# First chunk's last product from split operands, block by block of its weights

## The chip, the cores and the metric

The kernel runs on one core of a Trainium2 chip. The metric is device time in microseconds (us), the median of several executions. A core has five engines that matter here, each with its own queue that it works off in order: TensorE (PE, matmuls; PEld is its weight load), VectorE (DVE), ScalarE (ACT), GpSimd (POOL), and SyncE (SP), which issues the DMAs.

## What is computed

Attention with pooled keys and values, and a gated channel mix behind it, in float32 for 8 batches of 576 positions, 8 heads of 64:

```
k_p = k.reshape(B, H, Sp, pool, D).mean(axis=3)
v_p = v.reshape(B, H, Sp, pool, D).mean(axis=3)
attn = softmax(scale * np.matmul(q, k_p.transpose(0, 1, 3, 2)))
x = np.matmul(attn, v_p)
...
xk = mu_k * x + (1.0 - mu_k) * x_prev
xr = mu_r * x + (1.0 - mu_r) * x_prev
k = np.maximum(xk @ w_k, 0.0)
v = k * k @ w_v
r = 1.0 / (1.0 + np.exp(-(xr @ w_r)))
return (r * v).astype(np.float32)
```

x_prev is x one position earlier. The weights arrive as float64 words; w_k is 512 x 1024, w_v 1024 x 512, w_r 512 x 512.

## The kernel before

The 4608 positions are worked off in 12 chunks of 384, each made of three tiles of 128. A chunk's work: per tile the scores (`softmax`, L620), the normalized probabilities (px for the last 8 keys, L670; pm for the first 64, L676), their transposes on PE (`transposed` L695, `transposed_rest` L740 or L750); per pair of heads the product with the values (`attended`, L794) and the mixing with the position before (`shifted`: ScalarE L807, GpSimd copies L817 to L819, VectorE L826), which gives the operands of the channel mix, two per pair (m = 0 for k, 1 for r); eight blocks of the hidden product with w_k (`hidden`, L870), squared after relu; three gate products with w_r and a sigmoid (`gate`, L919, L926); three last products with w_v (`mixed`, L951), multiplied by the gate (L960) and stored (L964).

Most products are made from split operands: each number is the sum of a high part (rounded to the type float32r by a copy on ScalarE) and a low part (the rest, a subtraction), and three passes (high x high, low x high, high x low) stand for one float32 product. `x_parts` (L842 on ScalarE, L844 on GpSimd) splits the mixed operands, L893 and L895 split the squares (sh and sl), `split` (L491, L494) splits the weights. Chunk 0 alone (WHOLE) is computed from whole float32 operands, since the split weights don't exist yet: one matmul call, which the profile shows as two instructions. Weights are converted from float64 words to float32 by `convert` (L460 on ScalarE; L462, L464, L469 on VectorE), in place of the words, and split into high and low when chunk 0 is through with them: LOW_BY says whether VectorE (v) or GpSimd (g) makes the low part. SUM_BY says who adds up the pooled keys and values (t: PE, by L512; v or g: L501). BY_HEAD lists the tiles whose exponentials ScalarE makes head by head with the sum in the same step (L642); the others take a subtraction (L651), one exponential (L656) and a sum (L658).

`mixed` takes the tiles of a chunk one after the other, each with one PSUM bank ("mm", three of them), over the eight blocks of w_v. In chunk 0 the next tile's product may begin when the first has done its first block, and chunk 1's first hidden product when the third has.

The order in which every engine gets its instructions is set while the program is built, by the class `Order`: each function above is a generator that names the engine it needs next and waits for what it needs; a planner with assumed lengths takes, among those that are ready, the one with the earliest due time. Due times come from formulas at the end of the function (L968 to L998) less or plus an entry of the table EARLIER. What comes out is a fixed queue per engine; nothing is reordered on the chip. LOADS is the order of the first DMAs.

## Time and profile before

| | us |
|---|---|
| median of 3 executions | 631.29 (630.67 to 632.04) |
| the profiled execution | 631.28 |
| its span | 629.5 |
| busy in it: PE, DVE, ACT, POOL | 615.7, 402.1, 354.6, 208.2 |

The span is what the profiler saw from the first to the last instruction; 1.8 us of the execution lie outside it. In the page and the views, a row of a timeline starts with the start and the duration in us, then engine, line, operation, tile written <- tiles read, shape and count; in brackets the idle time of the engine ahead of it and what ended it. Matmuls overlap, so a matmul's own duration is longer than its share of PE: the step from one start to the next tells the share. The same holds for VectorE's rows, whose steps are some 0.08 us shorter than their durations.

### The profile page before, as it was taken

The page shows a single profiled execution, that of the slowest core. Times are in us where ns is not written, and L with a number is a line of the kernel's source. Part 1 is how long each engine was busy: PE and PEld are TensorE (multiplying, and loading weights), DVE is VectorE, ACT ScalarE, POOL GpSimd, SP SyncE. Part 2 cuts the span into 40 slices and gives each one's busy share as a digit, 9 for nine tenths or more (in the row PEclk, how much of TensorE's full clock was granted, in tenths as well). Part 3 has the DMA queues.
Part 4 walks back from the last instruction along what each step waited for, and adds up shares of the span by engine and source line. Part 5 has one row for each costly group of instructions (what it writes and reads, how often), then busy time and mean ns, then how long its engine had stood idle before and what let it go on. Part 6 is the DMA issues. An engine that isn't in the chain of part 4 may idle for free.

```text
span 629.5 us, 8993 instructions
## 1 busy us (share of the span) xinstructions
PE 615.7 (98%) x3210; PEld 533.1 (85%) x3210; DVE 402.1 (64%) x786; ACT 354.6 (56%) x778; POOL 208.2 (33%) x324
## 2 busy tenths in 40 slices
...
GB/s 315 340 403 171 34 35 51 35 76 142 94 51 158 59 51 51 2 143 108 18 18 51 42 187 55 3 18 56 133 98 33 35 18 33 18 2 33 18 2 50
DMA packets 34989, 50.92 MB, mean 81 GB/s; under 512 B 6528, under 2 KB 22912, under 8 KB 34944
## 3 DMA queue, kind: packets, MB, share of 16 engines
...
## 4 chain that ended last, share of the span: by engine, by line
PE 88%; DMA 6%; DVE 5%; SPq 1%; issue 0%; DVEq 0%
PE mm L951 32%; PE mm L870 29%; PE mm L919 14%; PE bank L794 5%; PE sc L620 5%; DMA got_wk<-in_w_k 4%; PE bank L695 2%; DMA got_wv<-in_w_v 1%; DVE tmp L464 1%; DVE got_wr L469 1%; PE bank L750 1%; SPq L421 0%; DVE got_wv L469 0%; DVE tmp L462 0%; DVE ptl L708 0%
## 5 line engine op out<-in xcount | busy, mean ns | idle before, releaser
L870 PE MATMUL mm<-xkh,w_k 128*128 128x384 f32 x704 | 182.3, 339 | 0.0
L951 PE MATMUL mm<-w_v,sh 128*128 128x512 f32 x528 | 171.7, 393 | 0.0
L870 PEld LDWEIGHTS mm<-xkh,w_k 128*128 128x128 f32 x704 | 125.6, 188 | 1.5 <-issue 0.6
L870 PE MATMUL mm<-xkl,w_k 128*128 128x384 f32 x352 | 118.0, 335 | 0.0
L951 PEld LDWEIGHTS mm<-w_v,sh 128*128 128x128 f32 x528 | 99.3, 188 | 19.5
L951 PE MATMUL mm<-w_v,sl 128*128 128x512 f32 x264 | 103.1, 390 | 0.0
L919 PE MATMUL mm<-w_r,xrh 128*128 128x512 f32 x264 | 86.3, 397 | 0.0
L807 ACT ACTIVATE t<-bank,om_sb 128x384 f32<-128x384 f32 x96 | 49.1, 580 | 46.7 <-PE bank L794 46.6
L893 ACT CAST sh<-rk 128x384 fp32r<-128x384 f32 x88 | 45.2, 513 | 51.9 <-DVE rk L887 51.4
L670 POOL TENSOR_TENSOR px<-e,sm 128x64 f32<-128x64 f32 x31 | 9.6, 310 | 189.8 <-DVE sm L664 189.8
L960 DVE TENSOR_TENSOR rs<-mm,rs 128x512 f32<-128x512 f32 x36 | 24.7, 687 | 74.7 <-PE mm L951 74.6
L826 DVE SCALAR_TENSOR_TENSOR xm<-bank,mu_sb,t 128x384 f32<-128x384 f32 x88 | 51.1, 612 | 31.8 <-POOL t L819 15.4
L895 DVE TENSOR_TENSOR sl<-rk,sh 128x384 fp32r<-128x384 f32 x88 | 53.3, 610 | 21.3 <-ACT sh L893 21.2
L870 PEld LDWEIGHTS mm<-xkl,w_k 128*128 128x128 f32 x352 | 66.1, 188 | 0.0
L887 DVE SCALAR_TENSOR_TENSOR rk<-mm,rk 128x384 f32<-128x384 f32 x88 | 48.5, 552 | 22.7 <-ACT rk L880 21.9
L501 POOL TENSOR_TENSOR stage<-stage 128x512 f32<-128x512 f32 (+5 forms) x60 | 52.9, 887 | 25.5 <-DMA stage<-in_vm 14.8
L844 POOL TENSOR_TENSOR xkl<-xm,xkh 128x384 fp32r<-128x384 f32 x44 | 45.5, 1034 | 48.0 <-ACT xkh L842 47.6
L919 PEld LDWEIGHTS mm<-w_r,xrh 128*128 128x128 f32 x264 | 49.7, 188 | 10.1
L951 PEld LDWEIGHTS mm<-w_v,sl 128*128 128x128 f32 x264 | 49.7, 188 | 8.9
L880 ACT ACTIVATE rk<-mm 128x384 f32<-128x384 f32 x88 | 42.9, 487 | 22.1 <-PE mm L870 21.1
L919 PE MATMUL mm<-w_r,xrl 128*128 128x512 f32 x132 | 51.5, 390 | 0.0
L620 PE MATMUL sc<-kbd,qs 128*128 128x144 f32 (+1 forms) x312 | 40.6, 289 | 5.4 <-ACT e L642 3.2
(120 smaller groups left out, 952.8 us busy)
## 6 DMA issues: line engine op xcount, KB each, us to landing
...
```

The lines of the kernel that those rows point to most:

```text
L501: nc_eng.tensor_tensor(out=st[:, :, :w], in0=st[:, :, :w], in1=st[:, :, w:2 * w], op=ALU.add)
L620: nc.tensor.matmul(out=halves[g // 2][o:o + n, 0, k:k + 2 * KEYS], lhsT=qs[:, g, o:o + n], rhs=kbd[b % 2][:, g, :], start=True, stop=True,)
L807: nc.scalar.activation(out=t[:, m, 1:n + 1], in_=xp, func=AF.Copy, scale=om_sb[:, m, g:g + 1])
L826: nc.vector.scalar_tensor_tensor(out=xm[:, :n], in0=xp, scalar=mu_sb[:, m, g:g + 1], in1=t[:, m, :n], op0=ALU.mult, op1=ALU.add,)
L844: nc.gpsimd.tensor_tensor(out=lo, in0=xm[:, :n], in1=hi, op=ALU.subtract)
L870: nc.tensor.matmul(out=hp, lhsT=w[:, o], rhs=x[:, ct, :n], start=(ct == 0 and k == 0), stop=(ct == NCT - 1 and k == len(terms) - 1),)
L880: nc.scalar.activation(out=rk[:, :n], in_=hp, func=AF.Relu)
L887: nc.vector.scalar_tensor_tensor(out=rk[:, :n], in0=hp, scalar=0.0, in1=rk[:, :n], op0=ALU.max, op1=ALU.mult)
L893: nc.scalar.copy(out=sh[:, :n], in_=rk[:, :n])
L895: nc.vector.tensor_tensor(out=operand("sl", c)[:, jt, :n], in0=rk[:, :n], in1=sh[:, :n], op=ALU.subtract)
L919: nc.tensor.matmul(out=bank, lhsT=x[:, ct, o], rhs=w, start=(ct == 0 and k == 0), stop=(ct == NCT - 1 and k == len(terms) - 1),)
L951: nc.tensor.matmul(out=bank, lhsT=s[:, o], rhs=w, start=(jt == 0 and k == 0), stop=(jt == NJT - 1 and k == len(terms) - 1),)
```

## The change

Chunk 0's last product is made from split operands like that of every other chunk: its squares are copied to sh (high) and the rest goes to sl, and the product takes three passes of split w_v. It takes the weights block by block: for each of the eight blocks the three tiles' products are added up, in three PSUM banks at once (`mixed_by_weights`); the output steps of a tile follow its last block (`put_out`). `second` holds the three passes. The hidden and the gate products of chunk 0 stay whole. w_v is split as soon as it is converted, with a tile of its own for each block; the conversion's last step writes to one of two new slots (fv), from which the split reads. Splits of w_k and w_r follow one another by the order of their loads alone, and chunk 1's first hidden product may begin when all of chunk 0's last product is issued. WBUFS falls by eight, for the eight tiles of w_v.

Beside that: tiles 1 and 3 also take their exponentials by head; two of the eight squares of chunk 0 go from ScalarE to VectorE; the low parts of w_r are all GpSimd's, those of w_v VectorE's but one; the sums of k0, v1 and v2 move (k0 to VectorE, v1 to GpSimd, v2 to PE); the order of the first loads and all due times are new.

Where instructions now stand, at three places. In these rows mm, bank and sc are PSUM banks, sh and sl the squares' parts, got_wr and w_r the converted and the split gate weights, w_v the split last weights, pm and px the probabilities, rows of x2 or x4 one row for several.

PE, at the start of chunk 0's last product, before (L740 and L695 transpose tile 5's probabilities, L919 is the gate, L620 the scores of tile 6):

```order
L740 MATMUL bank_113<-ident,pr_95 96x128 x2
L695 MATMUL bank_115<-ident,pm_90 128x128 x4
L919 MATMUL mm_117<-got_wr_249,xrh_363 128x512
L919 MATMUL mm_117<-got_wr_254,xrh_363 128x512
L919 MATMUL mm_117<-got_wr_278,xrh_363 128x512
L919 MATMUL mm_117<-got_wr_289,xrh_363 128x512
L620 MATMUL sc_112<-kbd_70,qs_104 128x144 x4
L951 MATMUL mm_118<-got_wv_293,sh_416 128x512
L951 MATMUL mm_118<-got_wv_306,sh_416 128x512
```

The same place now (L928 is the gate, L631 scores, L706 the transpose of tile 5's pm, L946 the product):

```order
L631 MATMUL sc_114<-kbd_70,qs_106 128x144 x4
L928 MATMUL mm_118<-got_wr_330,xrh_349 128x512
L928 MATMUL mm_118<-got_wr_335,xrh_349 128x512
L706 MATMUL bank_115<-ident,pm_91 128x128 x4
L946 MATMUL mm_120<-w_v_520,sh_426 128x512
L946 MATMUL mm_120<-w_v_520,sl_447 128x512
L946 MATMUL mm_120<-w_v_520,sh_426 128x512
L946 MATMUL mm_119<-w_v_520,sh_426 128x512
```

The transposes of tile 5's pm stood ahead of the last gate product and stand now directly ahead of chunk 0's last product; those of its px (L751) come after the product's seventh block. Further on, the four L805 groups of chunk 1 stand two ahead of the eighth block, one behind it, and one behind the first L881 rows of chunk 1.

VectorE, around tile 5's pm, before (L469 is the last conversion step of a block of w_v):

```order
L464 SCALAR_TENSOR_TENSOR tmp_101<-got_wv_306,tmp_101 128x512
L708 TENSOR_TENSOR ptl_463<-bank_114,pth_462 128x4x128
L670 TENSOR_TENSOR px_93<-e_89,sm_99 128x64
L469 SCALAR_TENSOR_TENSOR got_wv_306<-got_wv_306,tmp_101 128x512
L730 CAST pr_95<-px_93 128x2x32 x2
L676 TENSOR_TENSOR pm_90<-e_89,sm_99 128x512
```

The same place now (L466, L468, L477 are the conversion's steps, L503 the low part of a block of w_v, L512 adds up values, L687 is pm):

```order
L477 SCALAR_TENSOR_TENSOR fv_104<-got_wv_378,tmp_101 128x512
L503 TENSOR_TENSOR w_v_520<-fv_103,w_v_520 128x512
L512 TENSOR_TENSOR stage_108<-stage_108 128x2x256
L477 SCALAR_TENSOR_TENSOR fv_103<-got_wv_374,tmp_102 128x512
L669 TENSOR_REDUCE sm_99<-e_89 128x8
L466 TENSOR_SCALAR tmp_101<-tmp_101 128x512
L672 TENSOR_SCALAR sm_99<-sm_99 128x8
L675 RECIPROCAL sm_99<-sm_99 128x8
L468 SCALAR_TENSOR_TENSOR tmp_101<-got_wv_368,tmp_101 128x512
L681 TENSOR_TENSOR px_93<-e_89,sm_99 128x64
L512 TENSOR_TENSOR stage_108<-stage_108 128x2x128
L687 TENSOR_TENSOR pm_91<-e_89,sm_99 128x512
```

Before tile 5's pm stood behind the second conversion of w_v; now it stands behind the fourth, and behind the low parts of two blocks and all of chunk 0's squares.

GpSimd, at the operands of chunk 1, now (L855 makes low parts, k and r in turn, L681 and L687 are a tile's px and pm):

```order
L855 TENSOR_TENSOR xkl_808<-xm_85,xkh_807 128x384
L855 TENSOR_TENSOR xrl_829<-xm_83,xrh_828 128x384
L826 COPY t_81<-carry 128x2
L828 COPY carry<-t_81 128x2
L830 MEMSET t_81 128x2
L681 TENSOR_TENSOR px_93<-e_89,sm_99 128x64
L687 TENSOR_TENSOR pm_91<-e_89,sm_99 128x512
L826 COPY t_82<-carry 128x2
L828 COPY carry<-t_82 128x2
L830 MEMSET t_82 128x2
L855 TENSOR_TENSOR xkl_808<-xm_84,xkh_807 128x384
L855 TENSOR_TENSOR xkl_808<-xm_83,xkh_807 128x384
```

Two more low parts stand ahead of these rows and two behind, close together; before, the first pair stood alone between splits of w_k, well ahead of the rest.

The diff, with EARLIER cut to a row of each:

```
@@ -27,7 +27,7 @@
-WBUFS = 2 * NJT + NCT + 1
+WBUFS = NJT + NCT + 1
@@ -37,74 +37,74 @@
 REBASE = 2.0 ** -((1023 - 127) // 8)
 
 LOADS = (
-    "k0 k1 q1 q0 q2 wk0 c0 v0 v1 wk1 k3 r0 wk2 q3 wk3 wk4 v3 wk5 r1 q4 v2 wk6 wk7 wr0 wr1 q5 k2 wr2 "
-    "wr3 wv0 wv1 wv2 wv3 wv4 wv5 wv6 wv7 "
+    "k1 k0 q1 q0 wk0 v0 q2 v1 c0 wk1 k3 r0 wk2 q3 wk3 wk4 wk5 r1 v3 wk6 v2 k2 wk7 wr0 q4 wr1 wr2 wr3 "
+    "q5 wv0 wv1 wv2 wv3 wv4 wv5 wv6 wv7 "
 )
 
 SUM_BY = {
-    "k0": "t", "k1": "v", "v0": "t", "v1": "t", "r0": "t", "k2": "v", "k3": "v", "v2": "g", "v3": "v",
+    "k0": "v", "k1": "v", "v0": "t", "v1": "g", "r0": "t", "k2": "v", "k3": "v", "v2": "t", "v3": "v",
     "r1": "g",
 }
 
-NORM_BY = {0: "v", 1: "v", 2: "v", 3: "v", 4: "g", 6: "g", 5: "v"}
+NORM_BY = {0: "v", 1: "v", 2: "v", 3: "v", 4: "g", 6: "v", 5: "v"}
 WARMING = 4
 
-LOW_BY = {"k": "gvgvvvgv", "r": "gvgv", "v": "gvvggvgv"}
-BY_HEAD = (0, 2)
+LOW_BY = {"k": "gvgvvvgv", "r": "gggg", "v": "vvvvgvvv"}
+BY_HEAD = (0, 1, 2, 3)
 
 BESIDE = (1,)
-SQUARED_ON_ACT = 8
+SQUARED_ON_ACT = 6
 COPIES_ON_ACT = 0
 
 EARLIER = {
-    "transposed_rest 6": 4.1, "hidden 2 5": -6.4, "convert r 1": -3.5, "mixed 0 1": -9.9,
...
+    "transposed_rest 6": 28.2, "hidden 2 5": -0.7, "convert r 1": -3.1, "mixed 0 1": 8.4,
...
 }
-SPARE = 2.4
-SECOND = 13.3
+SPARE = 2.6
+SECOND = 15.4
 
@@ -285,7 +285,7 @@
 
     def operand(kind, c):
         if (kind, c) not in operands:
-            dtype = F32 if c in WHOLE and kind != "ptr" else F32R
+            dtype = F32 if c in WHOLE and kind not in ("ptr", "sh", "sl") else F32R
             operands[kind, c] = sb.tile(shapes[kind], dtype, name=f"{kind}_{c}", tag=kind)
         return operands[kind, c]
 
@@ -301,6 +301,7 @@
     slots("vq", 1, [REM, 2, D], F32R)
     slots("tmp", 2, [P, WP])
+    slots("fv", 2, [P, WP])
 
@@ -424,7 +425,10 @@
             return
         if kind[0] == "w":
             yield "sp", 0.6, False
-            got = sb.tile([P, 2 * WP], I32, name=f"got_{kind}{i}", tag="w", bufs=WBUFS)
+            own = kind[1] == "v"
+            got = sb.tile(
+                [P, 2 * WP], I32, name=f"got_{kind}{i}", tag=f"wv{i}" if own else "w", bufs=1 if own else WBUFS
+            )
             held["got", kind[1], i] = got
             nc.sync.dma_start(
                 out=got,
@@ -464,29 +468,34 @@
         nc.vector.scalar_tensor_tensor(
             out=t, in0=top, scalar=-0x80000000, in1=t, op0=ALU.bitwise_and, op1=ALU.bitwise_or
         )
+        to = got[:, :WP]
+        if kind == "v":
+            held["fv", i] = yield take("fv")
+            to = held["fv", i].bitcast(I32)
         yield dve(WP)
-        full[kind, i] = got[:, :WP].bitcast(F32)
+        full[kind, i] = to.bitcast(F32)
         nc.vector.scalar_tensor_tensor(
-            out=got[:, :WP], in0=low_word, scalar=29, in1=t,
+            out=to, in0=low_word, scalar=29, in1=t,
             op0=ALU.logical_shift_right, op1=ALU.bitwise_or,
         )
         order.give("tmp", ff)
         order.make(("full", kind, i))
 
-    order_of = [w[1:] for w in LOADS.split() if w[0] == "w"]
+    order_of = [w[1:] for w in LOADS.split() if w[0] == "w" and w[1] != "v"]
 
     def split(kind, i, *used):
 
         yield need(("full", kind, i), *used)
-        at = order_of.index(kind + str(i))
-        if at > WBUFS - 2 * NJT - NCT - 1:
-            before = order_of[at - (WBUFS - 2 * NJT - NCT)]
-            yield need(("parts", before[0], int(before[1:])))
-        if at:
-            yield need(("splitting", at - 1))
+        own = kind == "v"
+        if not own:
+            at = order_of.index(kind + str(i))
+            if at:
+                before = order_of[at - 1]
+                yield need(("parts", before[0], int(before[1:])))
         yield act(WP)
-        order.make(("splitting", at))
-        both = sb.tile([P, 2, WP], F32R, name=f"w_{kind}{i}", tag="w", bufs=WBUFS)
+        both = sb.tile(
+            [P, 2, WP], F32R, name=f"w_{kind}{i}", tag=f"wv{i}" if own else "w", bufs=1 if own else WBUFS
+        )
         high[kind, i], low[kind, i] = both[:, 0], both[:, 1]
         nc.scalar.copy(out=high[kind, i], in_=full[kind, i])
         v = LOW_BY[kind][i] == "v"
@@ -494,6 +503,8 @@
         (nc.vector if v else nc.gpsimd).tensor_tensor(
             out=low[kind, i], in0=full[kind, i], in1=high[kind, i], op=ALU.subtract
         )
+        if own:
+            order.give("fv", held.pop(("fv", i)))
         order.make(("parts", kind, i))
 
     def halve(nc_eng, st, cols, n):
@@ -872,10 +883,9 @@
                     start=(ct == 0 and k == 0), stop=(ct == NCT - 1 and k == len(terms) - 1),
                 )
         order.make(("hid", c, jt))
-        if c:
-            yield need(("mixed", c - 1), ("early", "sl", 0), ("early", "sl", 1))
+        yield need(("early", "sl", 0), ("early", "sl", 1), *([("mixed", c - 1)] if c else []))
         sh = operand("sh", c)[:, jt]
-        rk = sh if whole else (yield take("rk"))
+        rk = yield take("rk")
         yield act(n)
         nc.scalar.activation(out=rk[:, :n], in_=hp, func=AF.Relu)
         if c == 0 and jt < SQUARED_ON_ACT:
@@ -888,14 +898,13 @@
                 out=rk[:, :n], in0=hp, scalar=0.0, in1=rk[:, :n], op0=ALU.max, op1=ALU.mult
             )
             order.give("mm", bank)
-        if not whole:
-            yield act(n)
-            nc.scalar.copy(out=sh[:, :n], in_=rk[:, :n])
-            yield dve(n)
-            nc.vector.tensor_tensor(
-                out=operand("sl", c)[:, jt, :n], in0=rk[:, :n], in1=sh[:, :n], op=ALU.subtract
-            )
-            order.give("rk", rk)
+        yield act(n)
+        nc.scalar.copy(out=sh[:, :n], in_=rk[:, :n])
+        yield dve(n)
+        nc.vector.tensor_tensor(
+            out=operand("sl", c)[:, jt, :n], in0=rk[:, :n], in1=sh[:, :n], op=ALU.subtract
+        )
+        order.give("rk", rk)
         order.make(("s", c, jt))
 
     def gate(c, tt):
@@ -928,32 +937,17 @@
         held["rs", c, tt] = rs
         order.make(("gate", c, tt))
 
-    def mixed(c, tt):
-        whole = c in WHOLE
-        last = tt == CHUNKS[c] // P - 1
-        yield need(("gated", c))
-        if tt:
-            yield need(("mixing", c, tt - 1))
-        bank = yield take("mm")
+    def second(c, jt, tt, bank):
+
         o = slice(tt * P, (tt + 1) * P)
-        for jt in range(NJT):
-            yield need(("s", c, jt), ("full" if whole else "parts", "v", jt))
-            yield pe(DM, whole, 1 if whole else 3)
-            if jt == 0 and whole or jt == NJT - 1:
-                order.make(("mixing", c, tt))
-            if whole:
-                terms = [(operand("sh", c)[:, jt], full["v", jt])]
-            else:
-                h, l = high["v", jt], low["v", jt]
-                sh, sl = operand("sh", c)[:, jt], operand("sl", c)[:, jt]
-                terms = [(sh, h), (sl, h), (sh, l)]
-            for k, (s, w) in enumerate(terms):
-                nc.tensor.matmul(
-                    out=bank, lhsT=s[:, o], rhs=w,
-                    start=(jt == 0 and k == 0), stop=(jt == NJT - 1 and k == len(terms) - 1),
-                )
-        if last:
-            order.make(("mixed", c))
+        h, l = high["v", jt], low["v", jt]
+        sh, sl = operand("sh", c)[:, jt], operand("sl", c)[:, jt]
+        for k, (s, w) in enumerate([(sh, h), (sl, h), (sh, l)]):
+            nc.tensor.matmul(
+                out=bank, lhsT=s[:, o], rhs=w, start=(jt == 0 and k == 0), stop=(jt == NJT - 1 and k == 2)
+            )
+
+    def put_out(c, tt, bank):
         yield need(("gate", c, tt))
         rs = held.pop(("rs", c, tt))
         yield dve(DM, False)
@@ -964,6 +958,38 @@
         nc.sync.dma_start(out=out[at:at + P, :], in_=rs)
         order.now += 2.5
         order.give("rs", rs)
+
+    def mixed(c, tt):
+        yield need(("gated", c))
+        if tt:
+            yield need(("mixing", c, tt - 1))
+        bank = yield take("mm")
+        for jt in range(NJT):
+            yield need(("s", c, jt), ("parts", "v", jt))
+            yield pe(DM, False, 3)
+            if jt == NJT - 1:
+                order.make(("mixing", c, tt))
+            second(c, jt, tt, bank)
+        if tt == CHUNKS[c] // P - 1:
+            order.make(("mixed", c))
+        yield from put_out(c, tt, bank)
+
+    def mixed_by_weights(c):
+
+        yield need(("gated", c))
+        n = CHUNKS[c] // P
+        at = []
+        for _ in range(n):
+            at.append((yield take("mm")))
+        for jt in range(NJT):
+            yield need(("s", c, jt), ("parts", "v", jt))
+            for tt in range(n):
+                yield pe(DM, False, 3)
+                second(c, jt, tt, at[tt])
+                if jt == NJT - 1:
+                    order.add(0, put_out(c, tt, at[tt]))
+        order.make(("mixing", c, n - 1))
+        order.make(("mixed", c))
 
     order.add(-30, warm())
     order.add(-10, constants())
@@ -980,9 +1006,9 @@
         for i in range(n):
             at = {"k": FIRST + 2.6 * i - 4, "r": FIRST + 20 + 2 * i - 3, "v": FIRST + 28 + 2.5 * i}[kind]
             order.add(at, convert(kind, i))
-            used = {"k": [("hid", c, i) for c in WHOLE], "r": [("gated", c) for c in WHOLE], "v": [("mixed", c) for c in WHOLE]}[kind]
-            at = {"k": 2.1 * i - 4, "r": 15 + i, "v": 25 + 0.8 * i}[kind]
-            order.add(later + at, split(kind, i, *used))
+            used = {"k": [("hid", c, i) for c in WHOLE], "r": [("gated", c) for c in WHOLE], "v": []}[kind]
+            at = {"k": later + 2.1 * i - 4, "r": later + 15 + i, "v": FIRST + 28.1 + 2.5 * i}[kind]
+            order.add(at, split(kind, i, *used))
@@ -995,7 +1021,10 @@
             order.add(begin[c] + 0.0455 * n * jt / NJT, hidden(c, jt), 1.0 if c else 0.0)
         for tt in range(n // P):
             order.add(begin[c] + 0.0455 * n + 2.8 * tt, gate(c, tt))
-            order.add(begin[c] + (0.0455 + 0.022) * n + 5.5 * tt, mixed(c, tt))
+            if c not in WHOLE:
+                order.add(begin[c] + (0.0455 + 0.022) * n + 5.5 * tt, mixed(c, tt))
+        if c in WHOLE:
+            order.add(begin[c] + (0.0455 + 0.022) * n, mixed_by_weights(c))
 
```

88 rows, old and new, of the table EARLIER are left out of this document.

## The prediction

> **What bounds the kernel now.** I read the page first, then the chain that ended last in order of time, then busy time by stage, then the timelines of TensorE (PE), VectorE (DVE) and GpSimd (POOL) around the first chunk's last product. From the page, and busy time in five stages (columns: window, its length, busy us and instructions of PE, PEld, DVE, ACT, POOL, then granted clock, DMA share, GB/s):
>
> ```profile
> PE 615.7 (98%) x3210; PEld 533.1 (85%) x3210; DVE 402.1 (64%) x786; ACT 354.6 (56%) x778; POOL 208.2 (33%) x324
> 40.00:62.00 22.00, 20.94 (x86) 12.21 (x85) 21.87 (x46) 16.18 (x35) 2.70 (x4) 1.00 0.68 251
> 62.00:84.70 22.70, 22.46 (x80) 11.73 (x78) 22.00 (x45) 14.86 (x25) 6.32 (x8) 1.00 0.08 29
> 94.60:144.00 49.40, 49.37 (x263) 44.44 (x263) 34.00 (x62) 33.56 (x74) 28.18 (x32) 1.00 0.18 51
> 10.00:15.00 5.00, 1.81 (x14) 1.60 (x13) 4.48 (x14) 3.71 (x18) 0.00 (x0) 0.98 1.03 408
> 15.00:20.00 5.00, 5.00 (x33) 5.00 (x32) 4.93 (x20) 3.89 (x21) 0.00 (x0) 0.68 1.05 304
> ```
>
> There are two regimes. Behind 94.6 us PE is busy without a gap (49.37 of 49.40), so the end moves by exactly what PE loses or gains ahead. Between 40 and 84.7 us PE looks full too, but VectorE is as full (21.87 of 22.00): PE is fed by it. The PE timeline and the chain tell which rules where:
>
> ```profile
> 13.72 1.32 PE L620 MATMUL sc<-kbd,qs 128*128 128x144 f32 x8 [3.19 <-ACT e L642]
> ...
> 42.27 0.60 PE L695 MATMUL bank<-ident,pm 128*128 128x128 f32 x4
> 42.71 7.91 PE L870 MATMUL mm<-xkh,got_wk 128*128 128x384 f32 x24
> ...
> 60.92 3.70 PE L919 MATMUL mm<-got_wr,xrh 128*128 128x512 f32 x8 [0.25 <-DVE got_wr L469]
> ...
> 69.53 1.88 PE L951 MATMUL mm<-got_wv,sh 128*128 128x512 f32 x4
> 71.64 1.13 PE L951 MATMUL mm<-got_wv,sh 128*128 128x512 f32 x2 [0.23 <-DVE got_wv L469]
> ```
>
> ```profile
> 72.77 0.87 PE bank L794 x8
> 73.64 9.67 PE mm L951 x22
> 83.31 1.77 PE bank L794 x16
> 85.08 2.59 PE mm L951 x6
> 87.67 0.87 PE bank L794 x8
> 88.55 6.03 PE mm L951 x14
> 94.58 4.17 PE mm L870 x24
> ...
> 103.48 0.98 PE sc L620 x8
> ...
> 609.43 16.33 PE mm L951 x72
> ```
>
> The first chunk's last product starts at 69.53 and ends at 94.58. The last chunk computes the same product from split operands: 72 passes in 16.33.
>
> **The product itself.** From 69.53 to 94.58 are 25.05 us. In them lie four groups of L794 (0.87 + 1.77 + 0.87 = 3.51; 32 passes) and a wait of 0.23, so the product takes 21.3. In its new form it is 72 passes: 16.33. Gain: **5.0 us**, on PE, where nothing covers it.
>
> **When it can start.** PE's order now has the transposes of tile 5 right ahead of the product, and they need that tile's normalized probabilities, which VectorE writes (L676 before). So the start is set by how far VectorE has come. Its rows at that place, with those that give prices as the step from one start to the next (and two of GpSimd):
>
> ```profile
> 22.50 0.43 DVE L462 TENSOR_SCALAR tmp<-tmp 128x512 int32<-128x512 int32 x1 [1.26 <-ACT tmp L460]
> ...
> 27.02 0.42 DVE L462 TENSOR_SCALAR tmp<-tmp 128x512 int32<-128x512 int32 x1
> 27.35 0.75 DVE L651 TENSOR_TENSOR e<-sc,mx 128x576 f32<-128x576 f32 x1
> 28.02 0.68 DVE L464 SCALAR_TENSOR_TENSOR tmp<-got_wk,tmp 128x512 int32<-128x512 int32 x1
> 28.62 0.61 DVE L826 SCALAR_TENSOR_TENSOR xkh<-bank,mu_sb,t 128x384 f32<-128x384 f32 x1
> ...
> 45.64 1.67 DVE L469 SCALAR_TENSOR_TENSOR got_wr<-got_wr,tmp 128x512 int32<-128x512 int32 x1
> ...
> 63.20 0.69 DVE L676 TENSOR_TENSOR pm<-e,sm 128x512 f32<-128x512 f32 x1
> 63.80 0.22 DVE L732 TENSOR_TENSOR pr<-px,pr 128x64 fp32r<-128x64 f32 x1
> ...
> 107.16 1.02 DVE L895 TENSOR_TENSOR sl<-rk,sh 128x384 fp32r<-128x384 f32 x2
> 108.09 0.75 DVE L651 TENSOR_TENSOR e<-sc,mx 128x576 f32<-128x576 f32 x1
> 108.76 0.69 DVE L494 TENSOR_TENSOR w_v<-got_wv,w_v 128x512 fp32r<-128x512 f32 x1
> 109.36 0.55 DVE L887 SCALAR_TENSOR_TENSOR rk<-mm,rk 128x384 f32<-128x384 f32 x1
> 109.83 0.74 DVE L658 TENSOR_REDUCE sm<-e 128x8 f32<-128x576 f32 x1
> 110.49 0.68 DVE L494 TENSOR_TENSOR w_v<-got_wv,w_v 128x512 fp32r<-128x512 f32 x1
> ```
>
> ```profile
> 45.47 1.27 POOL L494 TENSOR_TENSOR w_k<-got_wk,w_k 128x512 fp32r<-128x512 f32 x1 [8.30 <-ACT w_k L491]
> 58.25 1.04 POOL L676 TENSOR_TENSOR pm<-e,sm 128x512 f32<-128x512 f32 x1
> ```
>
> Prices: a conversion's first step 0.33 and its other two 0.60 each, a weight's low half 0.60, a low half of the squares 0.46, a square 0.47, a sum of exponentials 0.66.
>
> Before, VectorE goes from its first mixing step (28.62) to the end of tile 5's pm (63.80) in 35.2 us. In the same stretch the changed order has, beyond that: eight low halves of the squares (3.7), two squares that leave ScalarE (0.9), two low halves of last weights (1.2), steps of three more conversions (3 x 0.33, 3 x 0.60 and 1 x 0.60: 3.4), and adding steps and attention halves that stood elsewhere (about 1.4 from rows of their size), less one sum of exponentials and two small copies (0.9): **+9.8 us** before rounding, 45.0 in all. The 35.2 hold about 2.6 beyond the bare steps; I keep them.
>
> Its first mixing step comes earlier. Tiles 1 and 3 take their exponentials by head on ScalarE, and VectorE has 1.15 us less to do ahead (three subtractions and a sum fewer, one conversion step and an adding step more): 27.5. If its waits went too (1.26 at 22.50), 26.4; if ScalarE's eight exponentials instead of one hold it up, still 28.6. I take 27.0, between the first two.
>
> So pm of tile 5 is done at 72.0, its transposes take 0.5, and the product starts at **72.5** instead of 69.53: **+3.0**. The cover that would hide VectorE's new work, PE's gates, runs out: the last gate weight is converted 34 us behind the first mixing step (31.9 of steps and 2), at 60.9 as before; PE then has the 8.6 us from 60.92 to 69.53 less tile 5's two transposes (0.7), is through at 68.8, and waits some 3 us.
>
> **The product's eight blocks** take 2.04 us each (16.33 / 8). Block 2's weights are ready 4.1 us of VectorE's steps behind pm of tile 5, and PE comes there 0.5 + 4.1 behind it. Block 7's are ready 16.4 of steps and about 1.0 of hold-ups behind, 17.4; PE comes 0.5 + 14.3 + 2.9 (scores 0.98, a transpose 0.2 and two L794 groups 1.77 stand before it) = 17.7. Both margins are under 0.5 us: VectorE and PE run neck and neck, and I charge nothing.
>
> **The hand-over to chunk 1.** Before, the first L794 group ran at 72.77, 22 us ahead of the chunk's first product. Now two groups come just ahead of block 7, one behind it, one inside the chunk's products. The operands of chunk 1 then come through a chain that is seen once early on:
>
> ```profile
> 75.38 0.62 DVE L826 SCALAR_TENSOR_TENSOR xm<-bank,mu_sb,t 128x384 f32<-128x384 f32 x1
> ```
>
> ```profile
> 76.03 0.51 ACT L842 CAST xkh<-xm 128x384 fp32r<-128x384 f32 x1 [0.65 <-DVE xm L826]
> ```
>
> ```profile
> 76.62 1.00 POOL L844 TENSOR_TENSOR xkl<-xm,xkh 128x384 fp32r<-128x384 f32 x1
> ```
>
> GpSimd makes one low half per 1.0 us, in the order k0, r0, k1, r1, a tile's px and pm (1.04 for pm, about 0.3 for px), k2, k3. From k0 to k3 these are 6.7 us with the carries. PE's work from where it needs k0 to where it needs k3 is 5.0 (one L794 group 0.87, seven groups of three L870 at 4.17/8 = 0.52, one transpose group 0.44, the step from 42.27 to 42.71). Stall: **+1.7**, between 1.0 (VectorE early) and 2.2 (late). Here it lies on the path: PE has nothing else queued.
>
> **Sum.** -5.0 (product) + 3.0 (start) + 0.2 (a transpose that now lies inside the product) - 0.2 (the wait that was inside it) + 1.7 (hand-over) = **-0.3**. Eight sums that leave PE for VectorE or GpSimd lie in the first 25 us, where PE waits anyway: nothing. Scores of two tiles and a transpose come earlier and are gone later: nothing. The tail behind the last product is unchanged. The profiled execution took 631.28 (629.5 span and 1.8 around it), the median is 631.29: **631.0 us**. About 0.2%, 1.3 us, can be told from no change here; so the forecast is no change.
>
> **Two rules weighed.** When GpSimd's 1.27 us subtraction ran at 45.47, VectorE's step at 45.64 took 1.67 instead of 0.68. The Trainium skill, SBUF — State Buffer, section Who interferes with whom, states why: the pair of ports that the two share is locked for a whole instruction and the second to come is blocked fully. By that rule each of the four long GpSimd subtractions now standing in VectorE's stretch up to block 7 could cost up to 1.3 us, 5.1 instead of the 3.6 that I keep for all hold-ups, and the time would be 632.5.
>
> The second is the clock: PE waited 3.19 us up to 13.72, and the granted clock was 0.68 from 15 to 20 us. The Trainium skill, TensorE: Matmul & The Clock Gate, Part 1, states that an idle window of about 3.4 us drops the clock to half; the trace fits this. It is a rival, below, since PE's new wait of about 3 us is of that length.
>
> **Rivals.**
>
> *VectorE runs freer (faster).* GpSimd adds up less in this stretch (one value sum moved to PE), so few of the 2.6 us of hold-ups may return, and ScalarE, 16.18 busy of 22.00, may keep pace. Against: ScalarE gets eight more copies there. With the first mixing step at 26.5 and bare steps of 42.3 and 0.6 of waits, the product starts at 69.9, the hand-over costs 1.0: -5.0 + 0.4 + 1.0 = -3.6, **627.7**. It counts as faster from a start at 71.5 on.
>
> *The clock drops (slower).* PE's wait before tile 5's transposes passes 3.2 us, and the product begins at a low clock: 5 us at 0.68 lose 1.6. With VectorE 1 us later, which brings the wait to 4: -0.3 + 1.0 + 1.6, **633.6**. For: the same length of wait did it at 13.72. Against: PE was sparsely used there (1.81 of 5.00), and is dense here.
>
> *Blocks wait for their weights (slower).* With margins under 0.5 us, a VectorE that loses 2 us more between block 2 and block 7 holds PE that long: **632.7**.
>
> **Numbers.** Forecast case 0.38; freer VectorE 0.36; clock 0.17; late weights 0.09. The range goes from the first rival's 627.6 (its bounds: start 69.9, hand-over 1.0) to 633.6. Within the forecast case alone: 630.0 to 632.5. Faster 0.36, same 0.38, slower 0.26.
>
> **What would show it.** Right: the L946 group starts between 71.5 and 73.5 and its 72 passes span 16 to 17 us of PE beside scores and L805; a PE wait of 2.5 to 3.5 us ends with VectorE's pm ahead of L706; small waits of the first L881 rows of chunk 1 for GpSimd's xkl; no gap behind 105. Wrong: a start before 71 or after 74, a granted clock under 0.95 between 65 and 80 us, or waits of single blocks for w_v over 1 us in all.

## The result and the profile after

The changed kernel takes 638.89 us in the median (638.32 to 639.74), the kernel before beside it 631.20: ratio 1.0113, 95% interval 1.0086 to 1.0140. That is slower, and outside the range. The profiled execution took 638.32 us, its span is 636.5, 7.0 more than before. (Each later set of runs had its own runs of the kernel before, 631.2 to 632.9 in the median; kernels of different sets are compared by their ratios to it, which can differ by up to 0.2% from the ratios of the medians shown.) Two executions of later kernels, 686.92 us (before_short) and 2190.81 us (warm_both), lie far above the others of their kernel and are left out of the times and ratios.

From the page, and busy time by stage of the changed kernel (columns as before):

```profile
PE 615.9 (97%) x3218; PEld 538.0 (85%) x3218; DVE 407.2 (64%) x799; ACT 362.1 (57%) x814; POOL 204.9 (32%) x321
```

```profile
10.00:15.00 5.00, 3.03 (x13) 2.68 (x13) 3.99 (x10) 2.60 (x18) 1.68 (x2) 1.00 1.05 389
...
62.00:84.70 22.70, 20.48 (x83) 13.72 (x81) 22.28 (x49) 15.79 (x24) 4.22 (x4) 1.00 0.26 87
74.00:96.00 22.00, 21.74 (x117) 18.33 (x115) 21.60 (x42) 13.79 (x25) 5.95 (x10) 1.00 0.11 38
96.00:107.60 11.60, 9.08 (x54) 7.71 (x53) 11.10 (x20) 9.13 (x20) 9.07 (x17) 1.00 0.26 89
```

Two of these stages in the kernel before:

```profile
74.00:96.00 22.00, 22.00 (x76) 11.92 (x75) 16.71 (x31) 13.49 (x25) 15.60 (x24) 1.00 0.07 25
96.00:107.60 11.60, 11.60 (x73) 11.53 (x71) 8.86 (x13) 8.42 (x22) 9.24 (x9) 1.00 0.21 69
```

From 74 to 107.6 us VectorE had 8.0 us free before (33.6 less 16.71 less 8.86) and has 0.9 now; PE was full and now has 2.8 free. The engine that is full has changed. The PE timeline of the changed kernel, with what ended its waits:

```profile
8.61 2.29 PE L631 MATMUL sc<-kbd,qs 128*128 128x144 f32 x8 [3.38 <-ACT kbd L548]
...
69.69 1.88 PE L928 MATMUL mm<-got_wr,xrh 128*128 128x512 f32 x4
73.64 0.66 PE L706 MATMUL bank<-ident,pm 128*128 128x128 f32 x4 [2.08 <-DVE pm L687]
74.06 0.47 PE L946 MATMUL mm<-w_v,sh 128*128 128x512 f32 x1
...
88.67 0.38 PE L751 MATMUL bank<-ident,pr 128*96 128x128 f32 x2
...
96.09 0.54 PE L881 MATMUL mm<-xkh,w_k 128*128 128x384 f32 x2
...
98.82 0.44 PE L881 MATMUL mm<-xkl,w_k 128*128 128x384 f32 x1 [0.77 <-POOL xkl L855]
```

The product starts at 74.06; seven blocks run without a gap to 88.67, 2.09 us each. Three rows of VectorE (first mixing step, tile 5's pm, a low half of w_k):

```profile
29.32 0.61 DVE L837 SCALAR_TENSOR_TENSOR xkh<-bank,mu_sb,t 128x384 f32<-128x384 f32 x1
...
72.90 0.69 DVE L687 TENSOR_TENSOR pm<-e,sm 128x512 f32<-128x512 f32 x1
...
101.90 1.41 DVE L503 TENSOR_TENSOR w_k<-got_wk,w_k 128x512 fp32r<-128x512 f32 x1
```

PE's waits between 60 and 108 us, and then behind 107 us (columns: us in total, times, longest); before, there were two of 0.2 us in the first stretch and none in the second:

```profile
PE bank L706 <- DVE pm L687: 2.1, 1, 2.1
PE mm L881 <- POOL xkl L855: 1.9, 3, 0.8
PE sc L631 <- DVE e L662: 0.8, 1, 0.8
PE mm L881 <- ACT xkh L853: 0.7, 1, 0.7
PE bank L805 <- ACT ptr L758: 0.3, 1, 0.3
```

```profile
PE bank L761 <- DVE pr L743: 1.0, 2, 0.7
PE mm L928 <- DVE rk L897: 0.5, 1, 0.5
```

Waits alone miss what is lost around them, so I split PE's time of both traces. Of each matmul's step to the next start, the usual step of its kind counts as work (lower quartile over the traces: 0.227 us for a split 128x512 pass, 0.429 for one of the two instructions of a whole one, 0.11 for a sum), and what goes beyond it as stall. The levels depend on that choice, the differences hardly:

| us | before | changed | difference |
|---|---|---|---|
| work | 597.5 | 591.2 | -6.3 |
| stalls to 30 us | 11.0 | 15.3 | +4.3 |
| 30 to 80 | 5.4 | 7.3 | +1.9 |
| 80 to 110 | 0.2 | 4.8 | +4.6 |
| behind 110 | 10.0 | 12.5 | +2.5 |

Of the work 2.0 are the sums that left PE (16 instructions of 0.12) and 4.3 the product. The differences add up to 7.0, the difference of the spans.

### The profile page after: what moved, and what is told of

The parts are those of the page before. It is cut to its first block, busy times and chain, and to the rows that moved or that the text cites. A ratio compares the mean times of both kernels' runs of the same rounds, so it can differ in the third digit from the quotient of the medians.

```text
span 636.5 us, 9057 instructions
## 1 busy us (share of the span) xinstructions
PE 615.9 (97%) x3218; PEld 538.0 (85%) x3218; DVE 407.2 (64%) x799; ACT 362.1 (57%) x814; POOL 204.9 (32%) x321
## 4 chain that ended last, share of the span: by engine, by line
PE 74%; DVE 16%; DMA 4%; ACT 3%; issue 1%; SPq 1%; POOL 0%; ACTq 0%; POOLq 0%; DVEq 0%
PE mm L946 28%; PE mm L881 24%; PE mm L928 12%; PE bank L805 5%; PE sc L631 4%; DVE sl L904 2%; DMA stage<-in_vm 2%; DVE stage L512 2%; PE bank L706 2%; DVE tmp L468 1%; DMA stage<-in_kT 1%; DVE rk L897 1%; DVE pr L741 1%; DVE mx L644 1%; DVE e L662 1%
## 5 line engine op out<-in xcount | busy, mean ns | idle before, releaser
L946 PE MATMUL mm<-w_v,sh 128*128 128x512 f32 x576 | 187.4, 393 | 0.0
L881 PE MATMUL mm<-xkh,w_k 128*128 128x384 f32 x704 | 182.3, 339 | 0.7 <-ACT xkh L853 0.7
L881 PEld LDWEIGHTS mm<-xkh,w_k 128*128 128x128 f32 x704 | 125.1, 188 | 2.7 <-ACT xkh L853 1.0
L946 PEld LDWEIGHTS mm<-w_v,sh 128*128 128x128 f32 x576 | 108.1, 188 | 21.9 <-DVE w_v L503 0.3
L881 PE MATMUL mm<-xkl,w_k 128*128 128x384 f32 x352 | 118.2, 336 | 1.9 <-POOL xkl L855 1.9
L946 PE MATMUL mm<-w_v,sl 128*128 128x512 f32 x288 | 112.3, 390 | 0.0
L928 PE MATMUL mm<-w_r,xrh 128*128 128x512 f32 x264 | 86.6, 397 | 0.5 <-DVE rk L897 0.5
L902 ACT CAST sh<-rk 128x384 fp32r<-128x384 f32 x96 | 49.2, 513 | 48.1 <-DVE rk L897 47.2
L904 DVE TENSOR_TENSOR sl<-rk,sh 128x384 fp32r<-128x384 f32 x96 | 56.8, 595 | 19.2 <-ACT sh L902 19.1
L881 PEld LDWEIGHTS mm<-xkl,w_k 128*128 128x128 f32 x352 | 66.1, 188 | 2.8 <-POOL xkl L855 2.8
L681 POOL TENSOR_TENSOR px<-e,sm 128x64 f32<-128x64 f32 x30 | 9.2, 307 | 173.8 <-DVE sm L675 172.2
L855 POOL TENSOR_TENSOR xkl<-xm,xkh 128x384 fp32r<-128x384 f32 x44 | 44.6, 1015 | 58.7 <-ACT xkh L853 58.3
L946 PEld LDWEIGHTS mm<-w_v,sl 128*128 128x128 f32 x288 | 54.2, 188 | 9.7
L890 ACT ACTIVATE rk<-mm 128x384 f32<-128x384 f32 x96 | 46.9, 489 | 25.8 <-PE mm L881 20.9
L928 PEld LDWEIGHTS mm<-w_r,xrh 128*128 128x128 f32 x264 | 49.7, 188 | 10.8 <-DVE rk L897 0.9
L512 POOL TENSOR_TENSOR stage<-stage 128x512 f32<-128x512 f32 (+5 forms) x54 | 47.2, 878 | 30.2 <-DMA stage<-in_vm 11.1
L928 PE MATMUL mm<-w_r,xrl 128*128 128x512 f32 x132 | 51.5, 390 | 0.0
L631 PE MATMUL sc<-kbd,qs 128*128 128x144 f32 (+1 forms) x312 | 42.6, 297 | 6.1 <-ACT kbd L548 3.4
```

The costliest lines, as they stand in the source:

```text
L512: nc_eng.tensor_tensor(out=st[:, :, :w], in0=st[:, :, :w], in1=st[:, :, w:2 * w], op=ALU.add)
L631: nc.tensor.matmul(out=halves[g // 2][o:o + n, 0, k:k + 2 * KEYS], lhsT=qs[:, g, o:o + n], rhs=kbd[b % 2][:, g, :], start=True, stop=True,)
L855: nc.gpsimd.tensor_tensor(out=lo, in0=xm[:, :n], in1=hi, op=ALU.subtract)
L881: nc.tensor.matmul(out=hp, lhsT=w[:, o], rhs=x[:, ct, :n], start=(ct == 0 and k == 0), stop=(ct == NCT - 1 and k == len(terms) - 1),)
L890: nc.scalar.activation(out=rk[:, :n], in_=hp, func=AF.Relu)
L902: nc.scalar.copy(out=sh[:, :n], in_=rk[:, :n])
```

## The experiments

Theory A, formed on this profile: VectorE's amount of work up to chunk 1's operands sets the time of the front (all that lies ahead of chunk 1's first product), and PE's passes there lie under its cover. The rival is the one that the sum was built on: PE's own passes are the path, and what it lost are three separate waits.

### Is PE's time in the product on the path?

**few_passes**, the product with a third of its passes:

```
-        for k, (s, w) in enumerate([(sh, h), (sl, h), (sh, l)]):
+        terms = [(sh, h), (sl, h), (sh, l)][: 1 if c in WHOLE else 3]
+        for k, (s, w) in enumerate(terms):
```

> The changed kernel in which chunk 0's last product keeps only its high-by-high pass: 24 matmuls instead of 72, so 48 x 0.227 = 10.9 us less of PE; nothing else on any engine is changed (this leaves out the two cross terms). Theory A (VectorE's work sets the time up to the hand-over, so PE's passes there are under cover): product starts at about 74, chunk 1's operands come when they came before, the gain is under 3 us: 636 to 639. Rival (PE's own work in the product is the path): the gain is most of the 10.9 us: about 628 to 630.

Measured: 638.15 us, ratio 1.0115 (1.0088 to 1.0142): 10.9 us less work on PE (the two cross terms are left out), no change of the ratio. The rival falls. The PE timeline shows where they went:

```profile
74.96 0.66 PE L706 MATMUL bank<-ident,pm 128*128 128x128 f32 x4 [2.07 <-DVE pm L687]
75.37 1.64 PE L947 MATMUL mm<-w_v,sh 128*128 128x512 f32 x6
77.71 2.34 PE L947 MATMUL mm<-w_v,sh 128*128 128x512 f32 x9 [0.70 <-ACT w_v L500]
85.22 2.93 PE L947 MATMUL mm<-w_v,sh 128*128 128x512 f32 x6 [5.17 <-ACT w_v L500]
```

The sixth block waits 5.17 us for its weights, and the seventh ends at about 87.9, where it ended at 88.7 in the changed kernel (here the product started 1.3 us later).

**before_short**, the same question put to the kernel before, two of eight blocks left out:

```
-            for k, (s, w) in enumerate(terms):
+            for k, (s, w) in enumerate(terms if jt > 1 or not whole else []):
...
-                    start=(jt == 0 and k == 0), stop=(jt == NJT - 1 and k == len(terms) - 1),
+                    start=(jt == (2 if whole else 0) and k == 0), stop=(jt == NJT - 1 and k == len(terms) - 1),
```

> The kernel before with 6 of the 8 blocks in chunk 0's last product: 18 of 24 fp32 matmuls, PE 21.3 / 4 = 5.3 us less, no step added or moved on any other engine (this leaves blocks 0 and 1 out of the product). As the prediction's step has it (PE's time in the product is uncovered): 5.3 us less than the kernel before beside it. Rival (VectorE's conversions and the operands of chunk 1 come no earlier, so PE waits for them): under 2.5 us less, with PE waits between 70 and 105 us.

Measured: 632.98 against 631.77 us, ratio 1.0005 (0.9987 to 1.0023). Nothing is gained here either. Its PE timeline:

```profile
72.75 1.10 PE L951 MATMUL mm<-got_wv,sh 128*128 128x512 f32 x2 [2.00 <-ACT w_k L491]
85.77 1.98 PE L951 MATMUL mm<-got_wv,sh 128*128 128x512 f32 x4 [1.35 <-DVE got_wv L469]
101.20 0.61 PE L870 MATMUL mm<-xkh,w_k 128*128 128x384 f32 x2 [0.63 <-DVE rk L887]
120.20 0.33 PE L750 MATMUL bank<-ident,pr 128*128 128x128 f32 x1 [0.47 <-DVE pr L732]
```

By the split used above, 5.2 us of work went and 6.1 of stalls came. So the kernel before was already fed just in time: its PE had no gap because its product was about as long as what fed it.

### Is it VectorE's amount of work?

**no_low_squares** leaves out the low halves of chunk 0's squares, **no_low_halves** those of the last weights too (in both PE keeps its passes and reads high halves instead); **double_low** computes the squares' low halves twice:

```
no_low_squares
+        if c not in WHOLE:
             nc.vector.tensor_tensor(
                 out=operand("sl", c)[:, jt, :n], in0=rk[:, :n], in1=sh[:, :n], op=ALU.subtract
             )
...
-        sh, sl = operand("sh", c)[:, jt], operand("sl", c)[:, jt]
+        sh = operand("sh", c)[:, jt]
+        sl = sh if c in WHOLE else operand("sl", c)[:, jt]
no_low_halves, beside that
+        if kind != "v":
             (nc.vector if v else nc.gpsimd).tensor_tensor(
                 out=low[kind, i], in0=full[kind, i], in1=high[kind, i], op=ALU.subtract
             )
...
-        h, l = high["v", jt], low["v", jt]
+        h = l = high["v", jt]
double_low
+        for _ in range(1 if c else 2):
             nc.vector.tensor_tensor(
                 out=operand("sl", c)[:, jt, :n], in0=rk[:, :n], in1=sh[:, :n], op=ALU.subtract
             )
```

> The changed kernel without VectorE's eight low halves of chunk 0's squares; the second pass of each block reads the high half in their place, so PE has the same 72 passes (this leaves out the low halves' share of the product). VectorE has 8 x 0.46 = 3.7 us less, one of them took 1.6 in the trace, so up to 4.8. Theory A (VectorE sets start and hand-over): everything up to the hand-over comes 3.5 to 4.5 us earlier: 634.5 to 635.5, and the stalls at chunk 1's first products shrink or stay. Rival (PE's path with the 2.08 us wait as the only loss): at most 2 us: 636.9 or more.

> The changed kernel without the eight low halves of chunk 0's squares and without the eight low halves of the last weights (this leaves them out of the products of all chunks; PE keeps its passes, reading high halves in their place). VectorE has 8 x 0.46 + 7 x 0.60 = 7.9 us less ahead of the hand-over, GpSimd one step of 1.3. Leaving out the squares' half alone gave 1.1 us. Theory A (VectorE's amount of work sets the front): the 4.2 us more come off nearly whole: 632.5 to 635. Rival (ScalarE's copies and the order on PE hold the front by now): 636.5 to 638.

> The changed kernel with each of the eight low halves of chunk 0's squares computed twice: VectorE has 8 x 0.46 = 3.7 us more ahead of the product's end, nothing else changes. Theory A (VectorE's amount of work sets the front): 3 to 4 us slower than the changed kernel, 642 to 643. Rival (VectorE waits there anyway, for ScalarE and PE): under 1.5 us.

| | VectorE | ratio (95%) | against the changed kernel |
|---|---|---|---|
| no_low_squares | -3.7 us | 1.0106 (1.0070 to 1.0141) | -0.4 us |
| no_low_halves | -7.9 | 1.0040 (1.0024 to 1.0056) | -4.6 |
| double_low | +4.7 | 1.0190 (1.0163 to 1.0217) | +4.9 |

(The last column is the difference of the ratios times 631 us.) The rows of the third give the 4.7: two steps go in 1.06 us (46.46 to the next start, 47.52), where one took 0.47, so the second costs 0.59.

```profile
46.46 1.14 DVE L905 TENSOR_TENSOR sl<-rk,sh 128x384 fp32r<-128x384 f32 x2
47.52 0.69 DVE L477 SCALAR_TENSOR_TENSOR got_wr<-got_wr,tmp 128x512 int32<-128x512 int32 x1
```

Added work costs about one for one, and removing all 7.9 us gives back 4.6; so A holds for the size of the effect. It missed the first step: 3.7 us off gave 0.4 (its runs spread from 635.4 to 641.6), not 3.5. In the trace, which is of the slowest of these runs, VectorE's pm of tile 5 came 1.8 us earlier, the last mixing steps 1.1; VectorE now waited 0.62, 0.33 and 0.31 for ScalarE between 50 and 56 us. And the product began at a low clock, behind a wait of 2.07 us:

```profile
70.00:80.00 10.00, 8.13 (x31) 6.71 (x32) 9.94 (x23) 5.18 (x11) 1.28 (x1) 0.83 0.16 54
```

Its first seven blocks took 16.0 us instead of 14.6. The later chunks lost 4.4 us more than in the changed kernel's trace, why is open. So this run doesn't measure what VectorE's 3.7 us are worth; ScalarE, the clock and the hand-over stand close behind VectorE.

### The stalls at the hand-over

**no_x_low** leaves GpSimd's low halves of chunk 1's operands out:

```
+        if c != 1:
             nc.gpsimd.tensor_tensor(out=lo, in0=xm[:, :n], in1=hi, op=ALU.subtract)
...
-                xh, xl = operand("xkh", c), operand("xkl", c)
+                xh, xl = operand("xkh", c), operand("xkh" if c == 1 else "xkl", c)
```

> The changed kernel without GpSimd's eight low halves of chunk 1's x operands; the products of chunk 1 read the high halves in their place (this leaves the low halves out of chunk 1). PE's passes and VectorE's steps stay. Theory L (PE's 4.5 us of stalls between 90 and 110 us are the latency of the hand-over chain, whose last link is GpSimd at 1.0 us a half): the three waits for xkl (0.77, 0.63, 0.47) go, the wait for xkh (0.65) stays, VectorE's step of 1.42 beside GpSimd at 101.9 falls to 0.7: 2 to 3 us less, 636 to 637. Rival (VectorE's amount of work sets the place of chunk 1's first product, and GpSimd only ends the wait): under 1 us, 638 or more.

Measured: 637.50 us, ratio 1.0075 (1.0049 to 1.0100), 2.4 us under the changed kernel by the ratios, whose intervals overlap: the size that theory L had. The waits for xkl are gone in its trace. Of the waits of chunk 1's products its PE timeline has only those for ScalarE's copies left:

```profile
101.90 1.31 PE L882 MATMUL mm<-xkh,w_k 128*128 128x384 f32 x6 [0.23 <-ACT xkh L853]
104.21 1.32 PE L882 MATMUL mm<-xkh,w_k 128*128 128x384 f32 x6 [0.99 <-ACT xkh L853]
```

And VectorE's low half of w_k, 1.41 us in the changed kernel, where GpSimd made a low half from 101.77 to 102.77, is back at its price:

```profile
102.40 0.68 DVE L503 TENSOR_TENSOR w_k<-got_wk,w_k 128x512 fp32r<-128x512 f32 x1
```

The Trainium skill, SBUF — State Buffer, section Who interferes with whom, says that the two lock each other out of a shared pair of ports; this pair of rows agrees, 0.73 us for one step.

**handover_early** tried to shorten the same chain by an earlier place, with one entry:

```
-    "transposed_rest 5": 22.5,
+    "transposed_rest 5": 1.5,
```

> The changed kernel with one table entry back at its value before (transposed_rest 5: 1.5 instead of 22.5). It brings the remainder transposes of tile 5 ahead of the product, and with them all four attention groups of chunk 1 between blocks 2 and 3 of the product instead of ahead of and behind block 8. Rival (the stalls at chunk 1's first products are the latency of the chain from a group over VectorE, ScalarE and GpSimd): the 4.5 us that PE lost between 90 and 110 us go, 634.5. Theory A (VectorE's amount of work up to chunk 1's operands sets the time, wherever the groups stand): what the hand-over saves, blocks of the product wait for weights: 637.5 to 639.5.

Measured: 656.87 us, ratio 1.0383 (1.0358 to 1.0408). Neither: the entry moved more than the four groups. Transposes of three tiles now stand ahead of the product's last block, PE waits for their probabilities, and the clock falls to 0.50 from 100 to 110 us. Its waits between 85 and 125 us:

```profile
PE bank L706 <- POOL pm L687: 5.9, 2, 3.4
PE mm L946 <- ACT w_v L500: 3.1, 1, 3.1
PE sc L631 <- DVE e L662: 1.8, 1, 1.8
PE bank L706 <- DVE pm L687: 1.7, 1, 1.7
```

So this run says nothing of the two theories.

### The start

**exp_light** makes ScalarE's rows of eight exponentials two of four heads each for tiles 1 and 2 (three heads in four then lack a maximum and a sum of their own; GpSimd fills the sums' tiles first), **by_head_back** takes two tiles off that way:

```
exp_light
-                for h in range(4):
+                for h in range(1 if i in (1, 2) else 4):
+                    m = KEYS * (4 if i in (1, 2) else 1)
...
by_head_back
-BY_HEAD = (0, 1, 2, 3)
+BY_HEAD = (0, 2)
```

> The changed kernel in which tiles 1 and 2 take their exponentials in two activations of four heads instead of eight of one head (this leaves out their own maximum and sum for three heads in four; two small GpSimd fills at the start are added). ScalarE's two rows of 2.5 us each become about 0.9. Theory S (three such rows, one behind the other, hold the first mixing step at 29.3 where the prediction put 27.0): ScalarE is through with tile 2 at about 18.5 instead of 21.7, the first mixing step comes between 26.5 and 28.2, the product starts 1 to 2.5 us earlier and the time falls by as much, to 636.5 to 638. Rival (VectorE is full there by itself): first mixing step at 28.8 or later, gain under 0.7.

> The changed kernel with BY_HEAD (0, 2) as before: tiles 1 and 3 take their exponentials through VectorE again, and ScalarE has one exponential instead of eight for each. Theory (ScalarE's rows of eight exponentials, 2.5 us a tile, now three in a row, hold the first mixing step at 29.3): the first mixing step comes at 28.5 or earlier, the product starts at 73.3 or earlier, 637 to 638. Rival (VectorE's 1.15 us more take the place): first mixing step 29.3 to 30, no gain: 638.5 to 640. Its planner also sets two attention groups ahead of block 5, which can lower the stalls behind the product.

exp_light: 638.68 us, ratio 1.0103 (1.0070 to 1.0137); each of the two rows took 1.08 us instead of 2.53, and the first mixing step came at 30.0, with no gain in time. Theory S falls. by_head_back: 649.88 us, ratio 1.0284 (1.0251 to 1.0317); the first mixing step came at 28.7, but another order of the front cost far more: the last block waits 5.27 and 2.73 us for its weights. It decides nothing.

What exp_light left is PE: in the changed kernel's start eight score matmuls take 2.29 us (8.61), behind a wait of 3.38 us that wasn't there before; in the kernel before they took 1.22 us. Three kernels fill such waits with matmuls whose result nobody reads:

```
warm_longer
-        for _ in range(WARMING):
-            yield "pe", 0.86, False
+        for k in range(WARMING + 3):
+            if k < WARMING:
+                yield "pe", 0.86, False
warm_both, beside that (before_warm: this alone, 12 of them, in the kernel before)
+        if i == 1:
+            idle = yield take("bank")
+            for _ in range(8):
+                nc.tensor.matmul(out=idle[:, :P], lhsT=ident, rhs=ident, start=True, stop=True)
+            order.give("bank", idle)
```

> The changed kernel with seven idle matmuls at the start instead of four, so that PE is busy from 1.5 to about 8 us instead of to 5.2; every other instruction stands as it stood. Theory C (the sum of a key half that left PE leaves it idle for 3.3 to 3.6 us ahead of the first scores, and PE then runs at half speed: eight score matmuls took 2.0 to 2.3 us instead of 1.2): scores take 1.2 us each from 8.5 us on, the first mixing step comes 0.5 to 1.5 us earlier than in the changed kernel's runs (28.5 to 30.7, mean 29.6), and the time falls by as much, 637.5 to 638.5. Rival (loads or VectorE set the start): first mixing step 29 to 30.5, no change.

> As warm_longer, and with eight more idle matmuls behind the scores of tile 1, which fill 1.8 us of the 2.0 to 2.3 that PE waits there. Theory C: PE stays at full speed up to 25 us, the first mixing step comes at 28 to 28.5, and the time falls by 1 to 2 us against the changed kernel: 637 to 638. Rival (loads or VectorE set the start): no change, 638.9.

> The kernel before with twelve idle matmuls behind the scores of tile 1, about 2.6 of the 3.2 us that PE waits there; every other instruction stands as it stood. Theory C: the clock stays at 1.0 behind 14 us, the 16 sums that took 3.55 us take 2.1, the first mixing step comes 0.5 to 1.4 us earlier than 28.6, and the time is 0.5 to 1.4 us under the kernel before. Rival (VectorE's 1.26 us wait for ScalarE at 22.5 and its own steps set the first mixing step): no change.

| | first mixing step | time | ratio (95%) |
|---|---|---|---|
| warm_longer | 29.2 | 638.18 | 1.0101 (1.0086 to 1.0117) |
| warm_both | 28.0 | 637.88 | 1.0098 (1.0081 to 1.0115) |
| before_warm | 27.4 | 631.23 | 0.9989 (0.9977 to 1.0000) |

PE in the start of warm_both:

```profile
8.58 1.22 PE L632 MATMUL sc<-kbd,qs 128*128 128x144 f32 x8 [2.14 <-ACT kbd L549]
9.64 1.14 PE L632 MATMUL mm<-kbd,qs 128*128 128x144 f32 x8
10.62 1.95 PE L639 MATMUL bank<-ident 128*128 128x128 f32 x16
13.68 1.25 PE L632 MATMUL sc<-kbd,qs 128*128 128x144 f32 x8 [1.12 <-ACT e L659]
```

Up to the first mixing step everything runs at full speed. That step comes 1.3 us earlier, and the product starts at 72.42. In before_warm it comes 1.2 us earlier. So a low clock delays the start by that much, in one trace of each kernel (other traces of the changed start spread from 28.5 to 30.7).

But this isn't what sets the two kernels apart. The kernel before has the low clock too (0.68 from 15 to 20 us). At full speed in both, the changed kernel's first mixing step is still 0.6 us later (28.0 against 27.4), where 1.6 us earlier was forecast. And warm_longer, which fills the wait that the moved sums left (0.83 instead of 3.38 us, scores in 1.25), gains nothing: its next wait, 2.91 us, lowers the clock instead (0.50 from 16 to 20 us). A difference stands in rows of VectorE. GpSimd, idle from 2.8 to 27.8 us in the kernel before, now adds up values there; in its time three rows of VectorE take longer than the same steps behind it:

```profile
13.24 2.94 POOL L512 TENSOR_TENSOR early_sl<-early_sl 128x512 f32<-128x512 f32 x3 [10.49 <-DMA early_sl<-in_vm]
```

```profile
14.12 0.75 DVE L649 TENSOR_SCALAR mx<-mx 128x8 f32<-128x8 f32 x1
15.21 0.52 DVE L681 TENSOR_TENSOR px<-e,sm 128x64 f32<-128x64 f32 x1
15.76 0.57 DVE L741 CAST pr<-px 128x64 fp32r<-128x64 f32 x2
...
18.11 0.12 DVE L649 TENSOR_SCALAR mx<-mx 128x8 f32<-128x8 f32 x1
18.23 0.22 DVE L681 TENSOR_TENSOR px<-e,sm 128x64 f32<-128x64 f32 x1
19.04 0.29 DVE L741 CAST pr<-px 128x64 fp32r<-128x64 f32 x2
```

That is 1.2 us, as much as the 1.15 us that VectorE was to have less to do. No run took this sum off GpSimd again, so the reading rests on the rows.

That the start passes on to the end is likely but not settled: 0.9 us less in the ratio, with overlapping intervals; before_warm, 0.7 us under the kernel before, has an interval that just touches 1. It is the fastest version tried, and not clearly faster. In warm_both's trace the product, too, began at a low clock, behind a wait of 2.07 us; two passes first took 0.85 us to the next start and later 0.46:

```profile
74.05 1.06 PE L952 MATMUL mm<-w_v,sh 128*128 128x512 f32 x2
...
77.31 0.62 PE L952 MATMUL mm<-w_v,sh 128*128 128x512 f32 x2
```

Its first seven blocks took 16.0 us instead of 14.6, which used up most of the 1.6 us that the product started earlier.

### The loss behind 110 us, and the tables

**late_back** gives the changed kernel the old entries of chunks 2 and 3, tiles 6 to 11 and SPARE; **late_alone** gives the new ones to the kernel before; **old_tables** has the new code with all tables and constants of before:

```
late_back (late_alone: the reverse, in the kernel before)
-    "transposed_rest 6": 28.2, "hidden 2 5": -0.7,
+    "transposed_rest 6": 4.1, "hidden 2 5": -6.4,
...
-SPARE = 2.6
+SPARE = 2.4
old_tables, beside all entries
-BY_HEAD = (0, 1, 2, 3)
+BY_HEAD = (0, 2)
...
-SECOND = 15.4
+SECOND = 13.3
```

> The changed kernel with the table entries of chunks 2 and 3 and of tiles 6 to 11, and the SPARE constant, as they stood before; the code and the entries of chunks 0 and 1 stay. In the changed kernel's trace PE's stalls of over 0.1 us behind 110 us add up to 3.4 us, in the kernel before to 1.0. Theory A (two separate losses: the front is filled by VectorE, and the late entries cost the rest): the late stalls go, about 2.4 us, and the front stays as it is: 636.5 us, product still starting at about 74.1. Rival (the late stalls follow from the late hand-over to chunk 1, whatever the entries): no change, 638.9.

> The kernel before with the changed entries for chunks 2 and 3 and tiles 6 to 11 and with SPARE 2.6; code and entries of chunks 0 and 1 as before. Theory B (these entries cost the 2.5 us behind 150 us by themselves): 633.7, the stalls lie behind 150 us as in the changed kernel. Rival (such entries fit only the order of the chunks ahead of them, and a mixture costs at its seam): 632 to 634 with the stalls between 100 and 140 us, as in the run with the old late entries. If they are harmless by themselves: 631.2, and the late loss comes from what the new front hands over.

> The changed code (product block by block from split operands, last weights split at once) with all tables and constants of the kernel before (LOADS, SUM_BY, NORM_BY, LOW_BY, BY_HEAD, SQUARED_ON_ACT, EARLIER, SPARE, SECOND). Theory A (VectorE's added splits fill the front under any order, the late stalls belong to the new tables): the front's loss of about 4 us stays and the late 2.4 us go: 634 to 637. Rival (the loss comes from the new order alone, the split product itself gains its 5 us): 626 to 629.

late_back: 640.28 us, ratio 1.0145 (1.0120 to 1.0170). late_alone: 644.37, 1.0189 (1.0164 to 1.0214). old_tables: 646.04, 1.0219 (1.0194 to 1.0245), where PE is busy for only 2.1 us between 40 and 50 (5.53 go in one wait). Theory A's number for the first, 636.5, is wrong. In late_back the three waits behind 150 us are gone, but others came at the seam, where old and new entries meet:

```profile
120.13 0.62 PE L881 MATMUL mm<-xkh,w_k 128*128 128x384 f32 x2 [0.49 <-DVE rk L897]
126.72 0.73 PE L928 MATMUL mm<-w_r,xrh 128*128 128x512 f32 x2 [0.62 <-POOL w_r L503]
```

In no_low_halves, whose first product of chunk 1 comes 3.5 us earlier, the old three stand as they stood:

```profile
PE bank L762 <- DVE pr L744: 1.0, 2, 0.7
PE mm L930 <- DVE rk L898: 0.5, 1, 0.5
```

So they belong to the new order of the later chunks, not to the late hand-over; and that order can't be exchanged alone, since late_alone has 12.0 us of stalls at its seam, from 140 to 200 us, where the kernel before has 2.0.

## Why the prediction was wrong, step by step

- **"Gain: 5.0 us, on PE, where nothing covers it": the step that failed.** The size was nearly right (2.09 us a block instead of 2.04; 4.3 us of work by the split). But VectorE's conversions and the operands of chunk 1 covered it: few_passes took 10.9 us more off PE and before_short 5.2, both for nothing. I read "busy without a gap" as "on the path". I counted VectorE up to block 7 and from there summed PE, though VectorE stayed full to 107.6 us.
- **VectorE's 45.0 us from the first mixing step to tile 5's pm:** right, 44.3 (29.32 to 73.59).
- **First mixing step at 27.0:** wrong, 29.3 (28.5 to 30.7 in the other runs with the same start). All of the start's miss (74.06 instead of 72.5) is here. The 1.15 us less to do on VectorE were lost again beside GpSimd's new sum (1.2 us), which the step "eight sums that leave PE ...: nothing" put at nothing; the 0.5 taken off for waits didn't come either. The low clock doesn't explain it: it cost 1.3 us, but the 28.62 that I started from held 1.2 of the same. The remaining 0.6 us stay open.
- **PE's wait ahead of tile 5's transposes, some 3 us:** 2.08, ended as said.
- **Blocks wait for nothing:** right.
- **Hand-over 1.7 us:** right in kind (ScalarE and GpSimd in turn, 2.6 us of waits), too small: 4.6 with what is lost around the waits. GpSimd's part is about 2.4 (no_x_low).
- **"The tail behind the last product is unchanged", no gap behind 105:** wrong by 2.5 us; the new due times of the later chunks bring waits of their own. I had looked at the diff's tables only up to the hand-over.
- **Rivals.** None came in the changed kernel's trace: VectorE didn't run freer, the granted clock stayed 1.00 around the product, no block waited. The port rule's 632.5 rested on VectorE's stretch being longer than 45.0, and it was shorter. The clock rule struck in the start. At the product I let it begin at a wait of 3.2 us; in warm_both and no_low_squares 2.07 us were enough, for 1.4 us.

What stays open: how much of the 7 us another order of the same code could give back. One entry cost 17 us (handover_early against the changed kernel), so the tables hide the mechanism's own worth; old_tables shows only that the old order doesn't suit it.
